# The gate's input turned by VectorE, plain fp32 gate products and the bias on VectorE, in a Fourier mixing and mixture-of-experts kernel

## The chip, the core and the metric

One NeuronCore of a Trainium2 chip runs the whole program. Its engines are TensorE (PE, with its weight loads, PEld), VectorE (DVE), ScalarE (ACT), GpSimd (POOL) and SP, which here only issues DMA transfers. The metric is device time in microseconds (us) of one execution. The kernel before takes 1477.63 us (median of 3 runs, 1476.96 to 1479.51).

## The reference

First a Fourier mixing of x (8 batches, 2496 positions, 256 channels), then a mixture of 8 experts whose routing fills each expert to its capacity in the order of the logits.

```python
X = np.fft.rfft(x, axis=1)
Yr = Xr @ w_r - Xi @ w_i + b_r
Yi = Xr @ w_i + Xi @ w_r + b_i
Yr = np.sign(Yr) * np.maximum(np.abs(Yr) - 0.01, 0.0)      # Yi alike
y = np.fft.irfft(Yr + 1j * Yi, n=2496, axis=1)
logits = y @ w_gate                                        # 19968 x 8
for idx in np.argsort(-logits.flatten()):                  # token, expert by falling logit
    ...                                                    # assign if the token is free and the expert not full
out[mask] = np.maximum(y[mask] @ w1[e], 0.0) @ w2[e]       # for each expert e, 2496 tokens
```

The logits decide the order, so they are computed to fp32 accuracy: in the kernel before by three bf16 parts of y and three of w_gate.

## The kernel before

**Stages of a batch.** The transform of 2496 = 39 x 64 points is done in parts. Stage 1 (line 1168) multiplies x by a matrix of 39 points and goes through DRAM (T1). Stage 3 (line 1208) does the 64 points, frequency by frequency. Then the weights: lines 1227 and 1235 form three products of the complex multiplication, each from a high and a low part of the input (xTh, xTl) and of the weights. VectorE adds them (line 1240) and shrinks them towards zero (1243 to 1246). Stage 4 (line 1256) and, after another trip through DRAM (T2), stage 5 (line 1294, in the last batch the plain fp32 form, line 1287) bring them back to y. Stage 5 works in 11 *units* of a batch, each 2 x 117 positions (the last 117 + 39) by 256 channels, in one PSUM tile. ScalarE copies the unit to yst (line 1296), SP stores it to YD.

**The gate.** TensorE transposes yst by an identity, four products a unit (line 1314), into a PSUM tile of its own (pT). ScalarE rounds that to bf16 (line 1318), VectorE takes the rest (1319), ScalarE (in the last batch VectorE, 1323) rounds the rest (1321), and GpSimd, in batches 1, 5 and 7 VectorE (the tuple YLV), takes the third part (1325). After every fourth unit and after the last, line 1336 multiplies: six rounds, in each of which up to four units stand in four column strips of 32 outputs of TensorE (8 experts x 3 parts of w_gate, 24 outputs). ScalarE copies the logits (1343), SP stores them to LG, unit by unit (1345).

**The bias.** In batches 0, 2, 3, 4 (the tuple BV) VectorE adds it to the products in PSUM (line 1229); in the others TensorE starts the sum with a product of ones and the bias in bf16 parts (line 1223).

**Routing and experts.** SP loads the logits of a batch in two transfers (line 410), VectorE adds the three parts for each pair of batches (417, 418) and takes the maximum. From the first four batches, 512 tokens of every expert are chosen early (`Router.early`), so that the experts can start on them while batches 5 to 7 are still transformed; eight closing rounds choose the rest, each in a chain of small VectorE operations, while TensorE multiplies for the experts (lines 710, 729, 730).

**What sets the order.** A planner written into the kernel (`Plan.run`) takes every task with a cost, a due position (`pos`, made of the numbers in Q) and a slack, fills the buffers and fixes the order of each engine when the program is built; engines then run their rows strictly in that order and wait by semaphores. PSUM has 8 banks, given out by QUOTA.

## Time and profile before

| | us |
|---|---|
| median of 3 runs | 1477.63 |
| profiled execution | 1477.74 |
| its span, first to last instruction | 1475.9 |
| TensorE busy | 1449.2 (98%) |
| VectorE busy | 1131.0 (77%) |
| ScalarE busy | 888.7 (60%) |
| GpSimd busy | 525.2 (36%) |

Busy time is the union of an engine's instructions. Records of matmuls overlap, since they are pipelined, so what one costs is read from the distance between starts and not from its length. The transforms and the gate fill the first 590 us, the experts the rest. TensorE's granted clock was 0.997 of full speed over the span.

### The profile page before, as it was taken

The page shows a single profiled execution, that of the slowest core. Times are in us where ns is not written, and L with a number is a line of the kernel's source. Part 1 is how long each engine was busy: PE and PEld are TensorE (multiplying, and loading weights), DVE is VectorE, ACT ScalarE, POOL GpSimd, SP SyncE. Part 2 cuts the span into 40 slices and gives each one's busy share as a digit, 9 for nine tenths or more (in the row PEclk, how much of TensorE's full clock was granted, in tenths as well). Part 3 has the DMA queues.
Part 4 walks back from the last instruction along what each step waited for, and adds up shares of the span by engine and source line. Part 5 has one row for each costly group of instructions (what it writes and reads, how often), then busy time and mean ns, then how long its engine had stood idle before and what let it go on. Part 6 is the DMA issues. An engine that isn't in the chain of part 4 may idle for free.

```text
span 1475.9 us, 32728 instructions
## 1 busy us (share of the span) xinstructions
PE 1449.2 (98%) x9135; PEld 1221.8 (83%) x9142; DVE 1131.0 (77%) x3234; ACT 888.7 (60%) x2092; POOL 525.2 (36%) x497
## 2 busy tenths in 40 slices
...
GB/s 199 205 316 247 281 213 293 226 283 231 232 231 251 205 172 193 159 119 104 169 136 110 169 109 180 123 161 138 133 118 141 113 118 143 113 67 42 24 22 30
DMA packets 221994, 240.50 MB, mean 163 GB/s; under 512 B 97598, under 2 KB 183787, under 8 KB 221803
## 3 DMA queue, kind: packets, MB, share of 16 engines
...
q14 instruction: 117, 0.96, 0.2%
...
## 4 chain that ended last, share of the span: by engine, by line
PE 85%; DVE 7%; ACT 3%; DMA 2%; issue 2%; SPq 1%; POOL 0%; POOLq 0%; DVEq 0%; ACTq 0%
PE b L710 23%; PE b L729 15%; PE b L730 8%; PE b L1227 7%; PE b L1256 5%; PE b L1208 4%; PE b L1235 4%; PE b L1168 3%; PE b L1294 3%; PE pt L710 3%; PE pt L729 2%; PE b L1314 2%; PE pt L730 1%; PE b L732 1%; PE b L1336 1%
## 5 line engine op out<-in xcount | busy, mean ns | idle before, releaser
L1038 POOL TENSOR_TENSOR s2l<-s2c,s2h 120x512 fp32r<-120x512 f32 (+1 forms) x84 | 105.0, 1256 | 257.9 <-ACT s2h L1035 246.9
L1227 PE MATMUL b<-wt,xTh 128*128 128x256 f32 x640 | 128.3, 297 | 0.9 <-ACT xTh L1214 0.9
L742 POOL DMA_INDIRECT out_dram<-xTh,li x64 | 65.2, 1018 | 158.5 <-DVE xTh L739 97.5
L1227 PEld LDWEIGHTS b<-wt,xTh 128*128 128x128 f32 x640 | 103.1, 191 | 6.5 <-issue 1.4
L742 POOL DMA_INDIRECT out_dram<-xTl,li x64 | 66.0, 1032 | 101.8 <-DVE xTl L739 56.9
L1325 POOL TENSOR_TENSOR yTl<-yr,yTh 128x468 bf16<-128x468 f32 (+1 forms) x55 | 61.3, 1115 | 102.5 <-ACT yTh L1321 79.1
L1208 PE MATMUL b<-FG,sh 128*128 128x128 f32 x640 | 92.2, 278 | 1.2 <-DVE sh L1189 1.2
L1227 PE MATMUL b<-wt,xTl 128*128 128x256 f32 x320 | 91.9, 287 | 1.3 <-DVE xTl L1217 1.3
L1208 PEld LDWEIGHTS b<-FG,sh 128*128 128x128 f32 x640 | 82.7, 191 | 6.3 <-issue 2.4
L738 ACT COPY xTh<-b 128x256 f32<-128x256 f32 x66 | 24.7, 374 | 95.2 <-PE b L730 76.6
L1256 PE MATMUL b<-y,FG 64*128 64x256 f32 x640 | 80.6, 390 | 0.1
L1240 DVE TENSOR_TENSOR y<-b,sx 128x512 f32<-128x512 f32 x80 | 54.9, 688 | 27.1 <-ACT sx L1238 24.2
L1256 PEld LDWEIGHTS b<-y,FG 64*128 64x128 f32 x640 | 58.3, 186 | 12.8 <-issue 1.3
L1168 PE MATMUL b<-xh,d 117*120 117x512 f32 (+1 forms) x154 | 64.2, 423 | 2.3 <-ACT xh L1035 2.2
L1294 PE MATMUL b<-s2h,d 120*117 120x512 f32 (+1 forms) x168 | 65.9, 399 | 0.0
L1319 DVE TENSOR_TENSOR yr<-b,yTh 128x468 f32<-128x468 f32 (+1 forms) x88 | 54.8, 625 | 13.9 <-ACT yTh L1318 13.0
L1038 DVE TENSOR_TENSOR xl<-xt,xh 117x512 fp32r<-117x512 f32 (+1 forms) x77 | 56.8, 747 | 11.0 <-ACT xh L1035 10.7
L1235 PE MATMUL b<-wt,xTh 128*128 128x256 f32 x320 | 63.4, 291 | 0.0
L1227 PEld LDWEIGHTS b<-wt,xTl 128*128 128x128 f32 x320 | 60.8, 190 | 3.1 <-DVE xTl L1217 2.7
...
L738 ACT COPY xTl<-b 128x256 f32<-128x256 f32 x68 | 25.4, 373 | 53.8 <-PE b L730 39.9
L739 DVE TENSOR_TENSOR xTh<-b,xTh 128x256 f32<-128x256 f32 x66 | 27.6, 418 | 38.8 <-ACT xTh L738 36.4
(1229 smaller groups left out, 5275.1 us busy)
## 6 DMA issues: line engine op xcount, KB each, us to landing
...
```

The costliest lines, as they stand in the source:

```text
L710: T.matmul(ps.t[:, 0:w], lhsT=W1[m].t[:, a, 128 * ft:128 * ft + 128], rhs=x_.t[:, 0:w], start=q + m == 0, stop=q + m == 3)
L729: T.matmul(ps.t, lhsT=hh.t[:, u:u + 128], rhs=W2[ft // 4].t[:, :, ft % 4], start=ft == 0, stop=False)
L730: T.matmul(ps.t[:, 0], lhsT=hl.t[:, u:u + 128], rhs=w_[0], start=False, stop=ft == 7)
L742: ins = P.indirect_dma_start(out=self.out, out_offset=bass.IndirectOffsetOnAxis(ap=oi.t[0:M, oo + t:oo + t + 1], axis=0), in_=o.t[0:M], in ...
L1038: lambda: eng.tensor_tensor(lb[1](), src(), hb[1](), op=OP.subtract), [srcb, hb[0]], [lb[0]], port=True)
L1168: T.matmul(ps.t[0:M], lhsT=d1[0:k_, a, 0:M], rhs=v.t[0:k_], start=i == 0, stop=i == 2)
L1208: T.matmul(ps.t[:, :, dt, i], lhsT=sh[k // 8].t[:, k % 8, 128 * dt:128 * dt + 128], rhs=at(Ft, k), start=True, stop=True)
L1227: T.matmul(pc.t[:, c], lhsT=a.t[:, 1 - c, dt], rhs=wt[2 - c].t[:, w, dt], start=not pb and dt == 0 and a is th and w == 0, stop=(c == 1 or ...
L1235: T.matmul(pa.t, lhsT=a.t[:, 2, dt], rhs=wt[0].t[:, w, dt], start=dt == 0 and a is th and w == 0, stop=dt == 1 and a is tl)
L1256: T.matmul(ps4[i].t[:, r], lhsT=at(Gt, 2 * (p - 1 + r) + c)[h], rhs=zs[r].t[h, c], start=c == 0, stop=c == 1)
L1294: T.matmul(ps.t[0:M, gs_], lhsT=d5[0:k_, a, 0:M], rhs=v.t[0:k_, gs_], start=i == 0, stop=i == 2)
L1325: yq.append(plan.add('V' if on else 'P', dve(2 * W) if on else pool(2 * W), pos + Q['t5'], lambda yh=yh, yl=yl, yr=yr, W=W, on=on: (V if o ...
```

## The change

VectorE turns each unit of y straight from the PSUM tile of stage 5 with one transpose of 32 x 32 blocks. After it, partition 32q + c holds channel c of every block of 32 channels, for the rows 32q to 32q + 31 of the unit; so the gate needs eight products a unit, one for each block of channels, with weights that are a block diagonal (the 32 x 8 piece of w_gate four times). They are plain fp32, 64 columns wide, up to four units side by side in column strips. The transposes on TensorE, their tile pT and the three bf16 parts of y and of w_gate are gone, and with them the additions of logit parts. Stage 5 writes 128 partitions, the last eleven zero. The logits lie in LG in another order: 24 stores instead of 88 and six loads a batch (`logit_parts`) instead of two. VectorE adds the bias in all batches; the bf16 bias and its preparation are gone. All numbers of the planner are new (of Q, P1X and SLACK two lines are shown), and buffers of the old gate serve the experts under the name ex.

```diff
-    D1 = np.zeros((117, 120)); D5 = np.zeros((120, 117))
+    D1 = np.zeros((117, 120)); D5 = np.zeros((120, 128))
...
-P1X = -8.145
+P1X = -9.511
...
-SLACK = dict(split=1.661, count=0.243, back=0.303, lists=0.8, os=1.437, hid=0.28, mm4=0, mm4l=0.807, tr=0.477, trl=2.345, gate=0.682, gatel=2.407)
+SLACK = dict(split=1.565, count=0.366, back=0.155, lists=0.715, os=1.464, hid=0, mm4=0.149, mm4l=1.175, tr=1.717, trl=3.296, gate=1.037, gatel=2.447)
...
-YLV = (1, 5, 7)
...
+TU = .62
...
-def load_logits(K, H, LG, LGb, b, lo, pos):
+def logit_parts(ML, LG, b):
     q, h = b // 2, b % 2
-    for t, r, n, w in ((H.ML[64 * h:64 * h + 64, :, JP * q:JP * q + JP], 0, 8, H.b_ML), (None, 8, 16, lo)):
-        K.dma(pos, lambda t=t, r=r, n=n: K.nc.sync.dma_start(lo.t[64 * h:64 * h + 64] if t is None else t, LG[b, r:r + n].rearrange("v (p j) -> p v j", j=JP)), 80e3, [LGb[b]], [w], run=156)
-
-
-def route_prep(K, H, q, lo, pos):
+    for c in range(3):
+        n = 22 if not c else 21
+        for k in range(2):
+            a, e = (JP * c, 32 * c + 32) if not k else (32 * c + 32, JP * c + JP)
+            if e > a: yield ML[64 * h + c:64 * h + c + 3 * n - 2:3, :, JP * q + a - JP * c:JP * q + e - JP * c], LG[b, a // 32].rearrange("e (n t) -> n e t", t=32)[0:n, :, a % 32:(e - 1) % 32 + 1]
+
+
+def load_logits(K, H, LG, LGb, b, pos):
+    def load():
+        for t, src in logit_parts(H.ML, LG, b): K.nc.sync.dma_start(t, src)
+    K.plan.add('SP', 2.4, pos, load, [LGb[b]], [H.b_ML], load=moved(80e3, 100, late=LATE['sp']))
+
+
+def route_prep(K, H, q, pos):
...
-    v(8 * JP, pos(), lambda: V.tensor_tensor(lo.t[:, 0:8], lo.t[:, 0:8], lo.t[:, 8:16], op=OP.add), [lo], [lo])
-    v(8 * JP, pos(), lambda: V.tensor_tensor(H.ML[:, :, J], H.ML[:, :, J], lo.t[:, 0:8], op=OP.add), [H.b_ML, lo], [H.b_ML])
...
-BV = (0, 2, 3, 4)
 BANKS = [f"b{i}" for i in range(7)] + ["pt0"]
-QUOTA = dict(p1=2, pz=2, p5=2, ps2=2, ps3=2, pa=1, ps4=2, pT=2, pL=1, psh=3, pl=1, pso=2, psx=1, pq=1)
+QUOTA = dict(p1=2, pz=2, p5=2, ps2=2, ps3=2, pa=1, ps4=2, pL=1, psh=3, pl=1, pso=2, psx=1, pq=1)
...
-    Bd1, Bd5, Bwg = K.one("d1", [117, 2, 120], F32R), K.one("d5", [120, 2, 117], F32R), K.one("wg", [128, 2, 32], BF)
+    Bd1, Bd5, Bwg = K.one("d1", [117, 2, 120], F32R), K.one("d5", [120, 2, 128], F32R), K.one("wg", [128, 8, 32])
...
-        r1, r2, bh = sb("y2", [128, 2, 256]), sb("xl", [128, 2, 256]), sb("s2h", [128, 2, 256], BF)
         plan.add('V', dve2(512), -1.4, lambda: V.tensor_scalar(Bbf.t, Bbt.t, LAM, None, op0=OP.add), [Bbt], [Bbf], after=after)
-        for q, (u, v) in enumerate(((Bbf, r1), (r1, r2))):
-            plan.add('V', dve2(512), 6.0, lambda u=u: V.tensor_copy(bh.t, u.t), [u], [bh], after=after)
-            plan.add('V', dve(512), 6.0, lambda u=u, v=v: V.tensor_tensor(v.t, u.t, bh.t, op=OP.subtract), [u, bh], [v], after=after)
-        plan.add('V', dve2(512), 6.0, lambda: V.tensor_scalar(Bbt.t, Bbf.t, idn[:, 0:1], None, op0=OP.mult), [Bbf, r1, Bidn], [Bbt], after=after)
-        plan.add('V', dve(512), 6.0, lambda: V.scalar_tensor_tensor(Bbt.t, r1.t, idn[:, 1:2], Bbt.t, op0=OP.mult, op1=OP.add), [Bbt, r1, r2, Bidn], [Bbt], after=after)
-        plan.add('V', dve(512), 6.0, lambda: V.scalar_tensor_tensor(Bbb.t, r2.t, idn[:, 2:3], Bbt.t, op0=OP.mult, op1=OP.add), [Bbt, r2, Bidn], [Bbb], after=after)
-        gs = sb("sx", [128, 2, 8])
-        plan.add('V', dve(64), -14, lambda: V.memset(wg, 0.0), [], [Bwg])
-        wl.append(add_dma(-79, lambda: nc.sync.dma_start(gs.t, w_gate.rearrange("(t p) e -> p t e", p=128)), 8e3, [], [gs], run=32, late=0))
-
-        g = gs
-        for k in range(3):
-            plan.add('V', dve(16), 5, lambda k=k, g=g: V.tensor_copy(wg[:, :, 8 * k:8 * k + 8], g.t), [g], [Bwg], after=after)
-            if k == 2: break
-            rest = sb("sx", [128, 2, 8])
-            plan.add('V', dve(16), 5, lambda k=k, g=g, rest=rest: V.tensor_tensor(rest.t, g.t, wg[:, :, 8 * k:8 * k + 8], op=OP.subtract), [g, Bwg], [rest], after=after)
-            g = rest
+        z_ = plan.add('V', dve(256), -14, lambda: V.memset(wg, 0.0), [], [Bwg])
+        for q in range(4): wl.append(add_dma(-79, lambda q=q: nc.sync.dma_start(wg[32 * q:32 * q + 32, :, 8 * q:8 * q + 8], w_gate.rearrange("(m c) e -> c m e", c=32)), 8e3, [], [Bwg], after=[z_], run=32, late=0))
...
-            pb = b not in BV
-
-            def mmc(th=th, tl=tl, pc=pc, pb=pb):
-                if pb: T.matmul(pc.t, lhsT=Bone.t, rhs=Bbb.t, start=True, stop=False)
+            def mmc(th=th, tl=tl, pc=pc):
                 for c in range(2):
                     for dt in range(2):
                         for a, w in ((th, 0), (th, 1), (tl, 0)):
-                            T.matmul(pc.t[:, c], lhsT=a.t[:, 1 - c, dt], rhs=wt[2 - c].t[:, w, dt], start=not pb and dt == 0 and a is th and w == 0, stop=(c == 1 or not pb) and dt == 1 and a is tl)
-            plan.add('T', 1.67 if pb else 1.44, pos + Q['m3'], mmc, [th_, tl_] + [Bone, Bbb] * pb + wt[1:], [pc], uses=[th, tl])
-            if not pb: plan.add('V', dve(512), pos + Q['zz'] - Q['ba'], lambda pc=pc: V.tensor_tensor(pc.t, pc.t, Bbf.t, op=OP.add), [pc, Bbf], [pc])
+                            T.matmul(pc.t[:, c], lhsT=a.t[:, 1 - c, dt], rhs=wt[2 - c].t[:, w, dt], start=dt == 0 and a is th and w == 0, stop=dt == 1 and a is tl)
+            plan.add('T', 1.44, pos + Q['m3'], mmc, [th_, tl_] + wt[1:], [pc], uses=[th, tl])
+            plan.add('V', dve(512), pos + Q['zz'] - Q['ba'], lambda pc=pc: V.tensor_tensor(pc.t, pc.t, Bbf.t, op=OP.add), [pc, Bbf], [pc])
...
-            ps = psum("p5", [117, 2, 256])
+            ps = psum("p5", [128, 2, 256])
...
-            W = 234 if u < 10 else 156
-            psT = psum("pT", [128, 2, 234])
-            yh, yl, yr = sb("yTh", [128, 2, 2, 234], BF), sb("yTl", [128, 2, 234], BF), sb("yr", [128, 2, 234])
-
-            def tr(u=u, st=st, psT=psT):
-                for i in range(2):
-                    M = 117 if u < 10 or i == 0 else 39
-                    for dt in range(2):
-                        T.transpose(psT.t[:, dt, 117 * i:117 * i + M], st.t[0:M, i, 128 * dt:128 * dt + 128], idn[0:M, 0:M])
-            plan.add('T', 0.44, pos + Q['t5'], tr, [st, Bidn], [psT], after=turn, slack=SLACK['trl' if b == NB - 1 else 'tr'])
-
-            y1_, y2_ = vb(), vb()
-            yt.append(plan.add('A', act(2 * W), pos + Q['t5'], lambda yh=yh, psT=psT, W=W: A.copy(yh.t[:, 0, :, 0:W], psT.t[:, :, 0:W]), [psT], [yh, y1_], after=yt[-1:]))
-            plan.add('V', dve(2 * W), pos + Q['t5'], lambda yh=yh, yr=yr, psT=psT, W=W: V.tensor_tensor(yr.t[:, :, 0:W], psT.t[:, :, 0:W], yh.t[:, 0, :, 0:W], op=OP.subtract), [psT, y1_], [yr])
-            if b < NB - 1:
-                plan.add('A', act(2 * W, False), pos + Q['t5'], lambda yh=yh, yr=yr, W=W: A.copy(yh.t[:, 1, :, 0:W], yr.t[:, :, 0:W]), [yr], [yh, y2_])
-            else:
-                plan.add('V', dve2(2 * W), pos + Q['t5'], lambda yh=yh, yr=yr, W=W: V.tensor_copy(yh.t[:, 1, :, 0:W], yr.t[:, :, 0:W]), [yr], [yh, y2_], port=True)
-            on = b in YLV
-            yq.append(plan.add('V' if on else 'P', dve(2 * W) if on else pool(2 * W), pos + Q['t5'], lambda yh=yh, yl=yl, yr=yr, W=W, on=on: (V if on else P).tensor_tensor(yl.t[:, :, 0:W], yr.t[:, :, 0:W], yh.t[:, 1, :, 0:W], op=OP.subtract), [yr, y2_], [yl], after=yq[-1:], port=True))
-
-            ys.append((yh, yl, W))
+            yT = sb("yT", [128, 2, 8, 32])
+            yt.append(plan.add('V', TU, pos + Q['t5'], lambda yT=yT, ps=ps: V.transpose(yT.t.rearrange("p g m r -> p (g m r)"), ps.t.rearrange("p g e -> p (g e)")), [ps], [yT], after=yt[-1:]))
+            ys.append(yT)
             if u % 4 < 3 and u < 10: continue
-            psL = psum("pL", [128, 234])
-            lg = sb("lgst", [128, 234])
-            u0 = u - len(ys) + 1
+            psL = psum("pL", [128, 2, 32])
+            lg = sb("lgst", [128, 2, 32])
+            u0, n = u - len(ys) + 1, len(ys)
 
             def gt(ys=ys, psL=psL):
-                for n in range(6):
+                for m in range(8):
                     for g, y in enumerate(ys):
-                        T.matmul(psL.t[32 * g:32 * g + 32, 0:y[2]], lhsT=wg[:, n % 2], rhs=y[1].t[:, n % 2, 0:y[2]] if n > 3 else y[0].t[:, n // 2, n % 2, 0:y[2]], start=n == 0, stop=n == 5)
-            plan.add('T', 0.47 + .12 * len(ys), pos + Q['g5'], gt, [t for y in ys for t in y[0:2]] + [Bwg], [psL], slack=SLACK['gatel' if b == NB - 1 else 'gate'])
-            for g, y in enumerate(ys):
-                w, M = y[2], 32
-                if w == 234:
-                    if g: continue
-                    M = 32 * sum(1 for y in ys if y[2] == 234)
-                plan.add('A', act(w), pos + .8, lambda g=g, M=M, w=w, lg=lg, psL=psL: A.copy(lg.t[32 * g:32 * g + M, 0:w], psL.t[32 * g:32 * g + M, 0:w]), [psL], [lg])
-            for g, y in enumerate(ys):
-                add_dma(pos + Q['lg'], lambda c0=234 * (u0 + g), g=g, w=y[2], lg=lg: nc.sync.dma_start(LG[b, :, c0:c0 + w], lg.t[32 * g:32 * g + 24, 0:w]), 22e3, [lg], [LGb[b]], run=936)
+                        T.matmul(psL.t[32 * g:32 * g + 32], lhsT=wg[:, m], rhs=y.t[:, :, m], start=m == 0, stop=m == 7)
+            plan.add('T', 1.1, pos + Q['g5'], gt, ys + [Bwg], [psL], slack=SLACK['gatel' if b == NB - 1 else 'gate'])
+            plan.add('A', act(64), pos + .8, lambda n=n, lg=lg, psL=psL: A.copy(lg.t[0:32 * n], psL.t[0:32 * n]), [psL], [lg])
+
+            add_dma(pos + Q['lg'], lambda n=n, c=64 * u0, lg=lg: nc.sync.dma_start(LG[b].rearrange("q e t -> (q e) t")[:, c:c + 64 * n].rearrange("k (g t) -> g k t", g=n), lg.t[0:32 * n].rearrange("k i t -> k (i t)")), 8e3 * n, [lg], [LGb[b]], run=256)
...
-    H.end = yq[-1:] if IOTA else []
+    H.end = yt[-1:] if IOTA else []
...
-    LG = dram.tile([B, 24, S], F32, name="LG")
+    LG = dram.tile([B, 4, 8, 704], F32, name="LG")
```

**TensorE, where units are transposed** (first stage-5 units of the first batches). Before, line 1314 is the transposes of a unit, line 1294 stage 5, line 1208 stage 3:

```order
L1294 MATMUL b_1655<-s2h_1487,d_96 117x512
L1294 MATMUL b_1655<-s2l_1511,d_96 117x512
L1294 MATMUL b_1655<-s2h_1487,d_96 117x512
L1314 MATMUL b_1662<-h_idn,yst_1561 128x117 x4
L1208 MATMUL b_1669<-FG_188,sh_1046 128x2x64 x4
L1294 MATMUL b_1682<-s2h_1564,d_96 117x512
L1294 MATMUL b_1682<-s2l_1577,d_96 117x512
```

In the changed kernel, with line 1280 for stage 5, 1158 for stage 1 and 1198 for stage 3, the same place reads:

```order
L1280 MATMUL b_1549<-s2h_1440,d_96 128x512
L1280 MATMUL b_1549<-s2l_1455,d_96 128x512
L1280 MATMUL b_1549<-s2h_1440,d_96 128x512
L1198 MATMUL b_1558<-FG_194,sh_1034 128x2x64 x4
L1280 MATMUL b_1574<-s2h_1508,d_96 128x512
L1280 MATMUL b_1574<-s2l_1519,d_96 128x512
L1280 MATMUL b_1574<-s2h_1508,d_96 128x512
L1158 MATMUL b_1586<-xh_1451,d_95 120x512
L1158 MATMUL b_1586<-xl_1537,d_95 120x512
```

The four transposes behind a stage-5 product are gone and nothing stands for them on TensorE.

**TensorE, the first gate.** Before, the bias product (line 1223), a group of weights products (1227) and the first of 24 pairs of weight load and gate product (1336):

```order
L1223 LDWEIGHTS h_ones
L1223 MATMUL b_1718<-bb,h_ones 128x512
L1227 MATMUL b_1718<-wt_305,xTh_1692 128x256 x2
L1227 MATMUL b_1718<-wt_305,xTl_1706 128x256
L1227 MATMUL b_1718<-wt_305,xTh_1692 128x256 x2
L1227 MATMUL b_1718<-wt_305,xTl_1706 128x256
L1227 MATMUL b_1718<-wt_291,xTh_1692 128x256 x2
L1227 MATMUL b_1718<-wt_291,xTl_1706 128x256
L1227 MATMUL b_1718<-wt_291,xTh_1692 128x256 x2
L1227 MATMUL b_1718<-wt_291,xTl_1706 128x256
L1336 LDWEIGHTS wg
L1336 MATMUL b_1750<-yTh_1413,wg 32x234
```

In the changed kernel, weights products (now line 1214) and the first four of 32 gate products (1303); the loads of fp32 weights are part of the rows:

```order
L1214 MATMUL b_1640<-wt_306,xTh_1591 128x256 x2
L1214 MATMUL b_1640<-wt_306,xTl_1612 128x256
L1214 MATMUL b_1640<-wt_306,xTh_1591 128x256 x2
L1214 MATMUL b_1640<-wt_306,xTl_1612 128x256
L1214 MATMUL b_1640<-wt_292,xTh_1591 128x256 x2
L1214 MATMUL b_1640<-wt_292,xTl_1612 128x256
L1214 MATMUL b_1640<-wt_292,xTh_1591 128x256 x2
L1214 MATMUL b_1640<-wt_292,xTl_1612 128x256
L1303 MATMUL b_1670<-yT_1371,wg 32x64
L1303 MATMUL b_1670<-yT_1415,wg 32x64
L1303 MATMUL b_1670<-yT_1510,wg 32x64
L1303 MATMUL b_1670<-yT_1563,wg 32x64
```

The bias product is gone from the head of the weights products, and a gate of four units is 32 rows over four inputs instead of 24 over eight.

**VectorE, batch 5's units beside batch 6's splits.** Before, with lines 1319 and 1325 for the parts of y, 1215 to 1218 for the splits of stage 3's output, 1240 for the sum of the weights products, the other lines early routing:

```order
L1319 TENSOR_TENSOR yr_6830<-b_6793,yTh_6825 128x468
L817 TENSOR_TENSOR ge_6747<-ge_6747,ga_6819 128x78
L549 TENSOR_SCALAR RD_6821<-ga_6771,wi_6800 128x78
L556 TENSOR_SCALAR Sme_6839<-h_io,wi_6800 128x512
L1218 TENSOR_TENSOR xTl_6778<-sx_6743,xTh_6745 128x256
L1325 TENSOR_TENSOR yTl_6848<-yr_6830,yTh_6825 128x468
L1215 TENSOR_TENSOR sx_6846<-b_6787,sx_6846 128x256
L1217 TENSOR_TENSOR xTl_6862<-b_6787,xTh_6850 128x512
L1218 TENSOR_TENSOR xTl_6862<-sx_6846,xTh_6850 128x256
L1240 TENSOR_TENSOR y_6880<-b_6802,sx_6743 128x512
L1319 TENSOR_TENSOR yr_6899<-b_6867,yTh_6878 128x468
```

In the changed kernel, with line 1293 for the block transpose, 1205 to 1208 for the splits, 1216 for the bias, 1230 for the shrinking, 651 for an expert's weights:

```order
L1227 TENSOR_TENSOR y_6215<-b_6133,sx_6034 128x512
L1293 STREAM_TRANSPOSE yT_6227<-b_6179 128x512
L1205 TENSOR_TENSOR sx_6229<-b_6210,sx_6229 128x256
L1207 TENSOR_TENSOR xTl_6242<-b_6210,xTh_6231 128x512
L1293 STREAM_TRANSPOSE yT_6250<-b_6236 128x512
L1208 TENSOR_TENSOR xTl_6242<-sx_6229,xTh_6231 128x256
L871 COPY h_lohi<-st_6131 128x1
L894 TENSOR_TENSOR rng<-h_lohi 128x1
L1230 SCALAR_TENSOR_TENSOR y_6215<-y_6215,y_6272 128x512
L1216 TENSOR_TENSOR b_6257<-b_6257,bf 128x512
L651 TENSOR_TENSOR sp_6286<-xt_6085,sp_6286 128x512 x2
```

One transpose stands where two subtractions stood, and an addition of the bias has come between a batch's products and their sum.

## Rows read from the trace of the kernel before

**Rows 1.** The page, part 1: busy us, share of span, instructions.

```profile
PE 1449.2 (98%) x9135; PEld 1221.8 (83%) x9142; DVE 1131.0 (77%) x3234; ACT 888.7 (60%) x2092; POOL 525.2 (36%) x497
```

**Rows 2.** Busy time by stretch; columns in the first row, (x) counts instructions.

```profile
core 0: us, PE busy (x) PEld busy (x) DVE busy (x) ACT busy (x) POOL busy (x), PEclk, DMA share, GB/s
0.00:394.00 394.00, 385.45 (x3008) 333.86 (x3014) 303.98 (x577) 326.05 (x725) 112.46 (x100) 1.00 0.78 251
394.00:599.00 205.00, 199.74 (x1550) 163.41 (x1552) 183.75 (x514) 167.36 (x419) 79.50 (x70) 1.00 0.66 205
700.00:800.00 100.00, 99.27 (x526) 80.63 (x525) 96.99 (x327) 57.42 (x152) 43.98 (x42) 1.00 0.45 143
```

**Rows 3.** TensorE's timeline around a gate: start, us, operation, count.

```profile
129.70 0.40 PE L1227 MATMUL b<-wt,xTh 128*128 128x256 f32 x2
129.94 0.28 PE L1227 MATMUL b<-wt,xTl 128*128 128x256 f32 x1
130.15 0.59 PE L1336 MATMUL b<-yTh,wg 128*32 128x234 bf16 x16
130.57 0.37 PE L1336 MATMUL b<-yTl,wg 128*32 128x234 bf16 x8
130.87 0.62 PE L1314 MATMUL b<-h_idn,yst 117*128 117x117 f32 x4
```

**Rows 4.** TensorE's timeline around the transposes of a unit.

```profile
105.21 0.56 PE L1314 MATMUL b<-h_idn,yst 117*128 117x117 f32 x4
105.64 0.58 PE L1227 MATMUL b<-wt,xTh 128*128 128x256 f32 x2
```

**Rows 5.** TensorE's timeline around a bias product (line 1223).

```profile
84.63 0.38 PE L1223 MATMUL b<-bb,h_ones 128*128 128x512 bf16 x1
84.85 0.50 PE L1227 MATMUL b<-wt,xTh 128*128 128x256 f32 x2
85.90 0.39 PE L1227 MATMUL b<-wt,xTl 128*128 128x256 f32 x1 [0.55 <-DVE xTl L1217]
```

**Rows 6.** Single lines: engine, operation, count: ns min/median/max, first and last start, forms.

```profile
L1314 PE MATMUL b<-h_idn,yst x352: 227/263/321, 105.2 to 577.1; 117*128 117x117 f32 x168, 39*128 39x39 f32 x8
...
L1336 PEld LDWEIGHTS <-wg x528: 92/97/100, 130.1 to 585.0; 128*32 128x32 bf16 x176
...
L1223 PEld LDWEIGHTS <-h_ones x40: 95/97/100, 84.5 to 523.5; 128*128 128x128 bf16 x40
```

**Rows 7.** The chain of waits in order of time: start, us, what (two stretches).

```profile
107.41 1.93 PE b L1256 x16
...
546.94 1.72 PE b L1287 x4
```

**Rows 8.** VectorE by line and form: count, busy us, mean ns, idle before.

```profile
L1319 DVE TENSOR_TENSOR yr<-b,yTh 128x468 f32<-128x468 f32 x80 | 51.1, 640 | 13.9 <-ACT yTh L1318 13.0 <-issue 0.5
...
L1229 DVE TENSOR_TENSOR b<-b,bf 128x512 f32<-128x512 f32 x40 | 27.7, 694 | 3.2 <-PE b L1227 3.1
...
L1325 DVE TENSOR_TENSOR yTl<-yr,yTh 128x468 bf16<-128x468 f32 x30 | 20.0, 670 | 1.5 <-PE b L1336 1.2
...
L1323 DVE CAST yTh<-yr 128x468 bf16<-128x468 f32 x10 | 3.9, 404 | 0.1
...
L418 DVE TENSOR_TENSOR h_ML<-h_ML,lo 128x312 f32<-128x312 f32 x4 | 2.8, 699 | 0.0
...
L417 DVE TENSOR_TENSOR lo<-lo 128x312 f32<-128x312 f32 x4 | 2.5, 616 | 0.2 <-DMA lo<-LG 0.2
...
L681 DVE STREAM_TRANSPOSE yTl<-yTh 128x256 f32<-128x256 f32 x4 | 1.7, 437 | 0.0
```

**Rows 9.** VectorE's waits, 0 to 590 us: total us, times, longest.

```profile
DVE sx L1215 <- ACT xTh L1214: 20.3, 33, 1.8
```

**Rows 10.** SP's logit transfers, by line (columns as in rows 6).

```profile
L1345 SPq DMA_DIRECT2D LG<-lgst x88: 289/362/1091, 131.4 to 587.0; - x88
...
L410 SPq DMA_DIRECT2D h_ML<-LG x8: 586/590/1102, 189.7 to 588.5; - x8
```

More of the change, by code (lines that the diff above doesn't have):

```diff
@@ L999, in phase_a @@
     k4 = lambda p, i: p // 2 * 4 + p % 2 + 2 * i
-    Bd1, Bd5, Bwg = K.one("d1", [117, 2, 120], F32R), K.one("d5", [120, 2, 117], F32R), K.one("wg", [128, 2, 32], BF)
+    Bd1, Bd5, Bwg = K.one("d1", [117, 2, 120], F32R), K.one("d5", [120, 2, 128], F32R), K.one("wg", [128, 8, 32])
     d1, d5, wg, idn, Bidn = Bd1.t, Bd5.t, Bwg.t, H.idn, H.b_idn
-    Bd5f = K.one("d5f", [120, 117])
-    Bml, Bone, Bbb = K.one("ml", [128, 1]), H.b_ones, K.one("bb", [128, 2, 256], BF)
+    Bd5f = K.one("d5f", [120, 128])
+    Bml, Bone = K.one("ml", [128, 1]), H.b_ones
     Bbf = K.one("bf", [128, 2, 256])
@@ L1064, in load_consts @@
             GX.append(add_dma(-80 + q, lambda k0=k0, k1=k1, G=G, o=o: nc.sync.dma_start(G.t[:, k0 - o:k1 - o], cG[:, k0:k1, :]), 65e3 * (k1 - k0), [], [G, BG_[q]], run=512 * (k1 - k0), late=0))
-        es = sb("yr", [120, 2, 117])
-        GX.append(add_dma(-70, lambda: nc.sync.dma_start(es.t, cD5.rearrange("p (h m) -> p h m", h=2)), 112e3, [], [es], run=936, k=15, late=12))
-        plan.add('V', dve(234), 9, lambda: V.tensor_copy(d5, es.t), [es], [Bd5])
+        es = sb("yT", [120, 2, 128])
+        GX.append(add_dma(-70, lambda: nc.sync.dma_start(es.t, cD5.rearrange("p (h m) -> p h m", h=2)), 112e3, [], [es], run=1024, k=15, late=12))
+        plan.add('V', dve(256), 9, lambda: V.tensor_copy(d5, es.t), [es], [Bd5])
         fg[:] = FX, GX
@@ L1265, in batch @@
         lg, ys = None, []
-        turn = yt[-1:] if b == NB - 1 else []
         for u in range(NU):
@@ L1286, in batch @@
                 if plain:
-                    plan.add('T', 4 * n / 2400, pos, lambda c_=c_, ps=ps, gs_=gs_, k_=k_, M=M: T.matmul(ps.t[0:M, gs_], lhsT=d5f[0:k_, 0:M], rhs=c_.t[0:k_, gs_], start=True, stop=True), [c_, Bd5f], [ps])
+                    plan.add('T', 4 * n / 2400, pos, lambda c_=c_, ps=ps, gs_=gs_, k_=k_: T.matmul(ps.t[:, gs_], lhsT=d5f[0:k_], rhs=c_.t[0:k_, gs_], start=True, stop=True), [c_, Bd5f], [ps])
                 else:
@@ L1290, in batch, with mm @@
                           (h, lambda h=h, gs_=gs_, k_=k_: h.t[0:k_, gs_]), (l, lambda l=l, gs_=gs_, k_=k_: l.t[0:k_, gs_]), 'A', 'P', n)
-                    def mm(h=h, l=l, ps=ps, gs_=gs_, k_=k_, M=M):
+                    def mm(h=h, l=l, ps=ps, gs_=gs_, k_=k_):
                         for i, (a, v) in enumerate(((0, h), (0, l), (1, h))):
-                            T.matmul(ps.t[0:M, gs_], lhsT=d5[0:k_, a, 0:M], rhs=v.t[0:k_, gs_], start=i == 0, stop=i == 2)
+                            T.matmul(ps.t[:, gs_], lhsT=d5[0:k_, a], rhs=v.t[0:k_, gs_], start=i == 0, stop=i == 2)
                     plan.add('T', 3 * (.004 + .000446 * n), pos, mm, [h, l, Bd5], [ps])
@@ L1346, in batch @@
             ys = []
-    last_sh, yt, yq = [], [], []
+    last_sh, yt = [], []
     head, wl, fg = [], [], []
```

30 lines of the change are left out of this document (12 added, 18 removed).

## The prediction

> **What bounds the kernel now.** I read the engine totals first, then the busy time by stretch, then TensorE's own timeline. TensorE is busy 98% of the span [rows 1]. By stretch it never rests for long: 385.45 of the first 394 us, 199.74 of the next 205, 99.27 of 100 later [rows 2]. No wait of TensorE stands among the long waits, so it is bound by the sum of what it is given, and an instruction taken off it shortens the span unless another engine is too full to follow. The reader should therefore look at the runner-up: VectorE is busy 303.98 of 394, then 183.75 of 205 us, and 96.99 of 100 in a later stretch in which TensorE still has 99.27 [rows 2]. The frequency transforms with the gate end at about 590 us; the change lies wholly before that.
>
> Busy times of single TensorE rows overlap, so I price work by the distance between starts. The gate of four units: the two weights products from 129.70 to 129.94 take 0.12 us each, the last one before the gate starts at 129.94 and so ends its turn at 130.06, the next work starts at 130.87: 0.81 us [rows 3]. Four transposes of a unit: 105.21 to 105.64, 0.43 us [rows 4]. A bias product: 84.63 to 84.85, 0.22 us [rows 5].
>
> **What leaves TensorE.** The trace has 352 transposes, four to a unit, so 88 units [rows 6]: 88 x 0.43 = 37.8 us; one unit in eleven is smaller, I take 37. It has 528 gate products [rows 6] in 24 groups (three to a batch, eight batches; a group of three units has as many rounds as one of four): 24 x 0.81 = 19.4 us. The 40 bias products (batches 1, 5, 6, 7) [rows 6] are 40 x 0.22 = 8.8 us at most. Here the cover matters: behind one of them a weights product stands 0.55 us for the low part of its input, which VectorE makes [rows 5]; there, without the bias, TensorE would only begin to wait sooner. Ends 0 and 8.8; I take 5. Sum: 37 + 19.4 + 5 = 61.4 us.
>
> **What comes to TensorE.** 24 groups of 8 fp32 products for each unit, 64 columns wide, 32 outputs high, four units in four column strips. The trace holds no fp32 product in a column strip, so I bound it. An fp32 product appears in the trace as two matmuls. The chain of waits has 4 matmuls of 512 columns in 1.72 us [rows 7]: 0.43 us for 512, hence 0.054 us for 64 columns; with a start-to-start allowance I use 0.056. With the strips side by side a group is 8 x 2 = 16 rounds of 0.056 = 0.90 us. The old gate shows the rest: six rounds of about 0.10 us are 0.6 of its 0.81, so entering and leaving strip mode costs 0.2. New group: 1.10 us. Do fp32 matmuls run side by side at all? In half-height tiles they do: 16 of 256 columns take 1.93 us, 0.12 each, where the 512-column rate gives 0.215 [rows 7]. Lower end 0.90, upper end 64 matmuls one after another, 64 x 0.056 + 0.2 = 3.8 us. I take 1.10, the value nearest to the rows that do overlap: 24 x 1.10 = 26.4 us. **Net on TensorE: 61.4 - 26.4 = 35.0 us less.** The stage-5 products now fill 128 outputs instead of 117; their columns, and so their turns, are the same.
>
> The weight loads of the gate are where a rule speaks against this change. The trace has 528 of them at 97 ns [rows 6], 24 in a group of 0.81 us: laid end to end they would be 2.3 us, so they are hidden behind running strips. The Trainium skill, TensorE: Matmul & The Clock Gate, Part 3 (Packing small matmuls), says that "LDWEIGHTS overlaps with in-flight MATMULs only when row_grp differs"; column strips share all rows, so by it no load would be hidden. The bf16 gate disagrees with that rule; for fp32 strips no run here shows it yet. The rule's result is the second rival.
>
> **VectorE.** It loses 88 subtractions of about 0.64 us, 33 of 0.67 (batches 1, 5, 7), 11 casts of 0.40, and eight additions of logit parts (2.5 + 2.8 us) [rows 8], together 56 + 22 + 4 + 5 = 87 us. It gains 40 additions of the bias at 0.694 [rows 8], 27.8 us, and 88 block transposes of 512 elements from PSUM. The nearest rows are a transpose of 256 elements from SBUF, 437 ns, and an addition of 512 elements from PSUM, 694 ns [rows 8]; ends 0.44 and 0.87 (twice the smaller one), I take 0.70: 61.6 us. Over the stage VectorE is even: +89 against -87.
>
> But it moves towards the end. In the later part, 394 to 599 us, in which about batches 4 to 7 are finished, the gain is 30 bias additions, 20.8 us, and 33 x 0.06 for the longer transposes; the loss is 22 subtractions (14.7), the casts (4) and half the logit additions (2.6): +1.5, so 185.2 us. The four batches in it lose 4 x 35/8 = 17.5 us of TensorE, so the stretch would be 187.5 us with VectorE 99% full. At the 97% that it reaches elsewhere without holding TensorE [rows 2] it needs 190.9: **3.4 us come back.** If it could not be filled beyond today's 183.75/205 = 90%, 206 us would be needed and the whole 17.5 would come back.
>
> **New waits.** ScalarE's copy of y and VectorE's transpose now read the same PSUM tile. Engines take turns on one: VectorE's line 1215 waited 33 times, 20.3 us, for ScalarE's line 1214 on the tile that both read [rows 9]. Behind a waiting transpose on VectorE stand the splits and bias additions for the next weights products. In exchange the subtraction that waited for ScalarE's copy of the old transposes goes. I cost this at 0, ends -4 and +6, hidden by the distance between transposing and gating (the planner puts whole products between them). The last batch's copies no longer follow one another through ScalarE and VectorE before the last gate; that only helps the start of the routing.
>
> **Transfers.** SP issues 24 logit stores instead of 88 (0.36 us each) and 48 loads instead of 16 (0.59) [rows 10]: 32 + 9 = 41 us of issuing before, 9 + 28 = 37 after if the new ones cost the same. The pieces are short, down to 28 bytes, but only the last batch's are waited for; ends 0 and 2 us, I take 0, because VectorE has other work then.
>
> **Sum.** The profiled execution took 1477.74 us (span 1475.9), 0.1 above the median of 1477.63, so no correction. 1477.74 - 35.0 + 3.4 = 1446.1: I forecast **1446 us**.
>
> **The rivals.** (1) *VectorE becomes the bound of the second half.* For it: 90% full already, 30 additions more there. Against: 97% elsewhere without harm. Price: 17.5 instead of 3.4 us come back: 1460 us. (2) *Weight loads are not hidden in fp32 strips.* Each of 16 rounds pays a load of 0.097 us beside its 0.056: 16 x 0.153 + 0.2 = 2.65 us a group, 63.6 in all, against 61.4 saved: 1477.74 + 2.2 + 3.4 = 1483 us, a little slower. Against it: the old gate's hidden loads. (3) *The strips run one after another in fp32*, at the gate itself: 3.8 us a group, 91 us, 1477.74 - 61.4 + 91 + 3.4 = 1511 us, slower. Both decide from 2.56 us a group (61.4/24); beyond that the change loses. Against (3): the fp32 half-height pairs. (4) *The work goes but the new order waits*: all but some microseconds lost to buffers and turns on PSUM, 1466 to 1480.
>
> **How the numbers follow.** Forecast 0.68, (1) 0.16, (2) 0.05, (3) 0.04, (4) 0.07. Within 0.2% (3 us) is what a measurement of this kernel can't tell from no change. Faster by more: the forecast, (1) and about half of (4), 0.88. Same: 0.03. Slower: (2), (3), and a little of (4), 0.09. The lower bound: all 8.8 us of bias, 37.8 of transposes, nothing returned: 1477.74 - 39.6 = 1438, less 4 for VectorE's freed waits: 1434. The upper end takes in rival (1) with the 6 us of turns on PSUM: 1466. Left out below about 0.06, above about 0.13.
>
> **What would show it.** In the changed profile: TensorE about 35 us less busy before the routing and still near 98%; a gate group of about 1.1 us between neighbours (2.6 or 3.8 show the rivals); transposes on VectorE near 0.70 us; ScalarE and GpSimd emptier by their copies and subtractions. The prediction is wrong if a gate group passes 2 us, if TensorE waits for VectorE by more than some 10 us in batches 5 to 7, or if the stretch after 600 us (now shifted) grows longer.

## The result and the profile after

The changed kernel took 1453.97 us (median of 4, 1451.99 to 1458.17) against 1478.49 before: a ratio of 0.9837, 95% interval 0.9818 to 0.9856. A second measurement of the same kernel gave 1453.31 us and 0.9842 (0.9827 to 0.9856). The forecast was 1446, with 1434 to 1466 as its range: the direction was right, and 7 to 8 us of the forecast gain of 32 are missing.

There are two profiled executions of the changed kernel: the first of 1458.17 us (span 1456.4), the slowest of its four, and one from the second measurement, 1453.30 us (span 1451.5), at the median. They differ mainly in two early stretches (busy time by stretch, columns as in [rows 2]; the first execution, then the second).

```profile
20.00:25.00 5.00, 4.28 (x38) 4.08 (x37) 1.69 (x4) 2.03 (x5) 0.00 (x0) 1.00 0.96 329
25.00:35.00 10.00, 7.09 (x28) 6.10 (x29) 4.12 (x8) 4.34 (x9) 0.00 (x0) 0.66 0.21 56
85.00:90.00 5.00, 5.00 (x27) 4.72 (x26) 2.14 (x6) 2.18 (x6) 0.00 (x0) 0.66 0.99 376
```

```profile
25.00:35.00 10.00, 7.80 (x46) 6.81 (x47) 5.97 (x11) 5.34 (x12) 0.00 (x0) 0.83 0.20 52
85.00:90.00 5.00, 4.83 (x41) 4.61 (x40) 4.54 (x10) 3.40 (x9) 0.00 (x0) 1.00 1.03 371
```

TensorE's granted clock, a mean of its two levels, is 1.00 at 20 us and 0.66 from 25 to 35 us in the first execution, 0.83 in the second. In between TensorE stood still for ScalarE's first split of batch 1, at about 24 us, 3.6 us long in the first and 3.1 in the second; ScalarE itself was waiting for the transfer of x. The first falls to 0.66 again at 85 us, after another wait at 82 us. At 0.66 instead of 0.83 over 10 us, and instead of 1.00 over 5, it lacks 1.7 + 1.7 = 3.4 us of full speed; the spans differ by 4.9. I therefore measure by the second execution, which stands at the median as the profiled run of before did. Its engine totals, to be laid beside [rows 1]:

```profile
PE 1418.9 (98%) x9630; PEld 1198.2 (83%) x9630; DVE 1118.2 (77%) x3210; ACT 813.1 (56%) x1919; POOL 470.8 (32%) x442
```

TensorE is busy 30.3 us less (1449.2 before). The span less this busy time is 32.6 us, 26.7 before. So 30.3 us of work went and 5.9 us of idle came: 24.4 us, which is the difference of the spans. The forecast had 35.0 and 3.4.

**The gate.** TensorE's timeline around the first gate of the second execution (start, us, operation, count), to be laid beside [rows 3]:

```profile
125.02 0.28 PE L1214 MATMUL b<-wt,xTl 128*128 128x256 f32 x1
125.22 1.10 PE L1303 MATMUL b<-yT,wg 128*32 128x64 f32 x64
126.25 0.51 PE L1222 MATMUL b<-wt,xTh 128*128 128x256 f32 x2
```

The product before the gate ends its 0.12 us turn at 125.14 and the next work starts at 126.25: 1.11 us, where 1.10 was forecast. The rivals had 2.65 and 3.8. A group has 64 weight loads, here by line in the first execution (columns as in [rows 6]):

```profile
L1303 PEld LDWEIGHTS b<-yT,wg x1408: 106/110/110, 129.3 to 570.0; 128*32 128x32 f32 x176
```

**VectorE.** By line and form, first execution, 0 to 600 us (count, busy, mean ns, idle before):

```profile
L1293 DVE STREAM_TRANSPOSE yT<-b 128x512 f32<-128x512 f32 x87 | 61.5, 709 | 8.3 <-PE b L1273 4.5 <-ACT yst L1282 1.8 <-PE b L1280 1.3
L1216 DVE TENSOR_TENSOR b<-b,bf 128x512 f32<-128x512 f32 x80 | 55.3, 692 | 12.5 <-PE b L1214 12.5
```

A block transpose is 709 ns; 0.70 was taken. Its idle time for ScalarE's copy of the same PSUM tile is 1.8 us, and TensorE waits for a transpose once, 0.5 us, so nothing here speaks against the 0 that was put down for the turns on PSUM. The SP queue's two logit transfers, to be laid beside [rows 10], were dearer than assumed:

```profile
L1307 SPq DMA_DIRECT2D LG<-lgst x24: 534/556/797, 131.7 to 570.8; - x24
...
L418 SPq DMA_DIRECT2D h_ML<-LG x48: 734/746/1043, 177.9 to 578.8; - x48
```

That is 13.3 + 35.8 = 49 us of issuing, not 37, and 41 before. No wait of TensorE names them.

**The new idle time.** TensorE's waits from 0 to 600 us (total us, times, longest); before first, the changed kernel (second execution) below it.

```profile
PE b L1168 <- ACT xh L1035: 2.2, 1, 2.2
PE pt L471 <- DVE cnt L466: 1.8, 2, 1.1
PE b L1227 <- DVE xTl L1217: 1.3, 3, 0.6
```

```profile
PE b L1214 <- DVE xTl L1207: 5.7, 11, 1.4
PE b L1158 <- ACT xh L1041: 4.1, 2, 3.1
PE b L1222 <- DVE xTl L1208: 1.8, 3, 1.4
```

The weights products now wait for the low part of their input, which VectorE subtracts: 5.7 us and eleven times, where it was 1.3 us and three times. The longest is read on both engines, TensorE first:

```profile
450.78 0.49 PE L1214 MATMUL b<-wt,xTh 128*128 128x256 f32 x2
452.64 0.39 PE L1214 MATMUL b<-wt,xTl 128*128 128x256 f32 x1 [1.38 <-DVE xTl L1207]
```

```profile
448.29 0.69 DVE L1216 TENSOR_TENSOR b<-b,bf 128x512 f32<-128x512 f32 x1
448.89 2.17 DVE L1230 SCALAR_TENSOR_TENSOR y<-y,y 128x512 f32<-128x512 f32 x1
450.98 0.68 DVE L1227 TENSOR_TENSOR y<-b,sx 128x512 f32<-128x512 f32 x1
451.58 0.41 DVE L1205 TENSOR_TENSOR sx<-b,sx 128x256 f32<-128x256 f32 x1
451.91 0.67 DVE L1207 TENSOR_TENSOR xTl<-b,xTh 128x512 fp32r<-128x512 f32 x1
```

```profile
449.21 1.29 POOL L1044 TENSOR_TENSOR s2l<-s2c,s2h 120x512 fp32r<-120x512 f32 x1
```

TensorE stands still because VectorE is behind: the subtraction at 451.91 comes after a bias addition and one operation, of line 1230, that took 2.17 us. GpSimd was subtracting beside it from 449.21 to 450.50 (the last line). The 35 operations of line 1230 that met no such subtraction took 0.68 us each; the last experiment comes back to this.

### The profile page after: what moved, and what is told of

Its sections match the earlier page's. It is cut to its first block, busy times and chain, and to the rows that moved or that the text cites. A ratio compares the mean times of both kernels' runs of the same rounds, so it can differ in the third digit from the quotient of the medians.

```text
span 1456.4 us, 33431 instructions
## 1 busy us (share of the span) xinstructions
PE 1422.1 (98%) x9630; PEld 1200.7 (82%) x9630; DVE 1119.2 (77%) x3210; ACT 813.3 (56%) x1919; POOL 473.3 (32%) x442
## 4 chain that ended last, share of the span: by engine, by line
PE 79%; DVE 13%; DMA 3%; ACT 2%; issue 2%; SPq 0%; POOL 0%; POOLq 0%; DVEq 0%; ACTq 0%
PE b L717 23%; PE b L736 15%; PE b L737 8%; PE b L1214 6%; PE b L1243 4%; PE b L1198 3%; PE pt L717 3%; PE b L1222 3%; PE b L1158 3%; PE pt L736 3%; PE b L1280 2%; PE pt L737 1%; PE b L1303 1%; DMA xt<-in_x_dram 1%; DVE xTl L1207 1%
## 5 line engine op out<-in xcount | busy, mean ns | idle before, releaser
L1214 PE MATMUL b<-wt,xTh 128*128 128x256 f32 x640 | 125.1, 291 | 0.0
L1293 DVE STREAM_TRANSPOSE yT<-b 128x512 f32<-128x512 f32 x87 | 61.5, 709 | 8.3 <-PE b L1273 4.5
L1280 PE MATMUL b<-s2h,d 120*128 120x512 f32 (+1 forms) x168 | 66.4, 404 | 0.0
L1216 DVE TENSOR_TENSOR b<-b,bf 128x512 f32<-128x512 f32 x80 | 55.3, 692 | 12.5 <-PE b L1214 12.5
L580 ACT ACTIVATE ajunk<-b,h_bs 128x156 bf16<-128x156 f32 x122 | 47.7, 391 | 27.5 <-PE b L575 23.1
L1282 ACT COPY yst<-b 117x512 f32<-117x512 f32 (+2 forms) x95 | 52.2, 557 | 19.4 <-DVE yT L1293 12.6
L1222 PE MATMUL b<-wt,xTh 128*128 128x256 f32 x320 | 62.9, 288 | 0.0
L717 PE MATMUL b<-yT,sh 128*128 128x512 f32 (+1 forms) x170 | 61.3, 384 | 0.0
```

Source lines behind the costliest of these rows:

```text
L717: T.matmul(ps.t[:, 0:w], lhsT=W1[m].t[:, a, 128 * ft:128 * ft + 128], rhs=x_.t[:, 0:w], start=q + m == 0, stop=q + m == 3)
L1214: T.matmul(pc.t[:, c], lhsT=a.t[:, 1 - c, dt], rhs=wt[2 - c].t[:, w, dt], start=dt == 0 and a is th and w == 0, stop=dt == 1 and a is tl)
L1222: T.matmul(pa.t, lhsT=a.t[:, 2, dt], rhs=wt[0].t[:, w, dt], start=dt == 0 and a is th and w == 0, stop=dt == 1 and a is tl)
L1280: T.matmul(ps.t[:, gs_], lhsT=d5[0:k_, a], rhs=v.t[0:k_, gs_], start=i == 0, stop=i == 2)
L1293: yt.append(plan.add('V', TU, pos + Q['t5'], lambda yT=yT, ps=ps: V.transpose(yT.t.rearrange("p g m r -> p (g m r)"), ps.t.rearrange("p g ...
```

## The experiments

Each run was measured beside the kernel before on the same chip. Where "the changed kernel" is the yardstick it is the second measurement, 1453.31 us; a cost is a difference of medians.

**The yardstick** (the changed kernel again).

> The changed kernel unchanged, as the yardstick of this call. Profiled first it took 1458.17 us, its median of four was 1453.97. Theory (waits that hang on the moment a transfer lands come and go): the median stays at 1452 to 1456, and the two longest early waits (3.9 us at 24 us, 2.2 us at 82 us) are shorter in another profile, while the waits of batch 7's weights products stay. Rival (the profile's 1458 is the truth): 1457 to 1459.

Measured 1453.31 us, 0.9842 (0.9827 to 0.9856). The theory held: both early waits are shorter (from start to start 3.4 instead of 3.9 us at 24 us, 1.4 instead of 2.2 at about 80 us) and the clock after them is higher, while the waits of the weights products are the same 5.7 and 1.8 us. The first profile's 1458 is the same kernel with longer early waits.

**Bias back on TensorE in four batches.** The table of its three addends occupies one of the five spare slots for expert data.

```
-            plan.add('V', dve(512), pos + Q['zz'] - Q['ba'], ...pc.t + Bbf.t...)
+            pb = b in (1, 5, 6, 7)
+                if pb: T.matmul(pc.t, lhsT=Bone.t, rhs=Bbb.t, start=True, stop=False)
+            if not pb: plan.add('V', dve(512), pos + Q['zz'] - Q['ba'], ...pc.t + Bbf.t...)
```

> The changed kernel with the bias of batches 1, 5, 6 and 7 again made by a TensorE product, as in the kernel before; VectorE adds it in batches 0, 2, 3, 4 only. Theory (removing these 40 products was worth nothing, because the products behind them wait for the low part from VectorE anyway, and VectorE's 30 additions after 394 us cost more waits): no slower than the changed kernel, 1448 to 1455 us, and the weights products of batch 7 wait at least 3 us less. Rival (the bias products cost what the forecast put down, 5 us, up to 8.8): 1459 to 1463 us.

Measured 1454.75 us, 0.9837 (0.9823 to 0.9850): no difference. The totals of its profile, and two of TensorE's waits to 600 us (its lines 1225 and 1215 are 1214 and 1207 of the changed kernel):

```profile
PE 1423.7 (98%) x9667; PEld 1202.2 (83%) x9670; DVE 1096.2 (75%) x3177; ACT 813.4 (56%) x1919; POOL 470.9 (32%) x442
```

```profile
PE b L1225 <- DVE xTl L1215: 3.7, 8, 1.2
...
PE b L1225 <- ACT xTh L1212: 0.8, 1, 0.8
```

TensorE is busy 4.8 us more, close to the 5 that the forecast had put down for these products, and idle 1453.2 - 1423.7 = 29.5 us instead of 32.6. From 440 to 540 us, about where batch 7 is, the waits for low parts fall by 2.3 us (4.8 to 2.5), short of the 3 that the theory wanted. This run moves work on two engines: TensorE has 40 products more, VectorE 22 us less to do. It shows that the exchange is worth nothing that the noise lets one see; what the products cost by themselves is read from the run without any bias, below.

**Bias back on TensorE in batch 7 alone** (the same edit with `b in (7,)`).

> The changed kernel with the bias of batch 7 alone again by TensorE: 10 products come back to it, 10 additions of 0.69 us leave VectorE between about 456 and 530 us. Theory (the waits of batch 7 are VectorE's doing): 3 to 5 us faster than the changed kernel, 1449 to 1451. Rival (each bias product costs TensorE its 0.13 to 0.22 us and the waits stay): 1 to 2 us slower.

Measured 1453.58 us, 0.9837 (0.9823 to 0.9850): neither. The waits of these products for the low part are 5.7 us as before; the one at 451 us is 1.2 instead of 1.4 us, and one of 1.5 us has grown at 503 us. The 1.8 us of the neighbouring products (line 1222) are gone. So batch 7's own ten additions account for about a third of its waits at most (4.8 to 3.2 us from 440 to 540 us), and ten products on TensorE stand against that.

**The old tables of numbers in the changed kernel** (`P1X`, `SLACK` and `Q` as before).

> The changed kernel with the three tables of planner numbers of the kernel before (lead, slack and due times). The work is the changed kernel's, only its order is other. Theory (the gain is the work taken from TensorE, the tables are worth a few us): 1456 to 1466 us, still faster than before. Rival (the gain comes from the new numbers): 1475 or more.

Measured 1458.50 us, 0.9862 (0.9847 to 0.9877). Of the 25 us the new numbers are worth about 5, the work 20. The new numbers in the kernel before were not run.

**The gate, one strip after another.**

```
-                for m in range(8):
-                    for g, y in enumerate(ys):
+                for g, y in enumerate(ys):
+                    for m in range(8):
```

> The changed kernel with the 64 TensorE records of a gate group in another order: all eight products of one unit (one column strip), then of the next, instead of the four strips in turn. Nothing else moves. Theory (a group costs 1.03 us because the four strips run side by side): products of one strip follow one another at 0.056 us or more, a group takes 3.6 us, 24 groups add some 62 us: 1510 to 1520 us, slower than before; if their weight loads of 0.11 us show as well, 7 us a group and up to 1600. Rival (an fp32 product of 64 columns is cheap by itself, strips or not): 1453 to 1458.

Measured 1488.41 us, 1.0063 (1.0048 to 1.0077): slower than before. The same place of TensorE's timeline:

```profile
125.83 0.28 PE L1214 MATMUL b<-wt,xTl 128*128 128x256 f32 x1
126.04 3.18 PE L1303 MATMUL b<-yT,wg 128*32 128x64 f32 x64
129.15 0.51 PE L1222 MATMUL b<-wt,xTh 128*128 128x256 f32 x2
```

A group goes from 1.03 to 3.11 us between first start and the next work; the records of one strip start 0.056 us apart, the price taken in the prediction. I had expected 3.6, and 62 us on top: start-to-start at the borders of strips falls to 0.025 to 0.030 us, so the next strip begins beside the last. The groups add 43.5 us on TensorE and the time 35. Of the rivals that were to make the change a loss, the one with strips that run one after another would thus have been real; the order of two loops decides it.

**The gate twice** (`for m in [*range(8), *range(8)]`).

> The changed kernel with each gate group computed twice, the second pass over the first. Theory (what TensorE is given sets the time): 0.94 us more in each of 24 groups, 22 us less what waits can hide, 1470 to 1476. Rival (TensorE's waits for VectorE hide the gate): under 1465.

Measured 1471.04 us, 0.9955 (0.9938 to 0.9972): 17.7 us for 23.1 us of groups. Each of the 24 groups takes 1.92 instead of 1.03 us, which is 21.4 us in all; the rest is waits inside a few of them.

**Every block transpose of one half made twice.**

```
+ [V.transpose(yT..., ps...) for _ in range(1 + (b in (0, 1, 2, 3)))]     (the other run: 4, 5, 6, 7)
```

> The changed kernel with each block transpose of batches 0 to 3 made twice by VectorE: 44 x 0.70 = 31 us more on VectorE between about 100 and 360 us, nothing on TensorE. Theory (VectorE at 82% has room there): 0 to 5 us, 1453 to 1458. Rival (VectorE is on the path all through): 1470 or more.

Measured 1470.89 us, 0.9943 (0.9930 to 0.9956). The theory fell, and the rival's number came: 17.6 us for 31 us of VectorE, in the half in which VectorE is 80% busy in the changed kernel (first line, columns as in [rows 2]). TensorE's waits for line 1207 rise from 5.7 to 12.9 us, and their number from 11 to 23 (second line, of this run).

```profile
0.00:394.00 394.00, 382.88 (x3379) 333.12 (x3380) 314.16 (x655) 292.55 (x646) 74.66 (x63) 1.00 0.81 253
```

```profile
PE b L1214 <- DVE xTl L1207: 12.9, 23, 1.4
```

> The changed kernel with each block transpose of batches 4 to 7 made twice by VectorE: 44 x 0.70 = 31 us more between about 360 and 570 us, nothing on TensorE. Theory (VectorE is 89% busy there and its fullness returns part of the gain): the stretch of 186 us holds 165 us of VectorE's work, 196 do not fit, so at least 10 us, and up to 30, come on top: 1464 to 1483. Rival (VectorE has room here as well, and the waits come from the order): under 1458.

Measured 1475.13 us, 0.9978 (0.9968 to 0.9987): 21.8 us for 31.

**The same in the second half, told to the planner** (`TU * (1 + (b > 3))` as its length).

> As the run with the block transposes of batches 4 to 7 made twice, but the planner is told their length of 1.24 us, so that it can put other work around them. Theory (VectorE stands at an edge: what is taken from it is worth 0.1 us per us, what is put on it 0.6 to 0.7, since 165 + 31 us don't fit into that stretch): the cost stays at least 10 us over the changed kernel, 1464 or more. Rival (the 22 us came from an order planned for the shorter transposes): under 1460.

Measured 1470.37 us, 0.9954 (0.9940 to 0.9968): 17.1 us. Planning around it gives 4.8 back (3.5 by the ratios to the kernel before); the other 17 us remain although the planner knew the length. One of its stretches, and below it that of the changed kernel:

```profile
510.00:540.00 30.00, 25.43 (x243) 19.22 (x242) 28.52 (x70) 15.83 (x48) 14.25 (x14) 0.89 0.50 154
```

```profile
510.00:540.00 30.00, 29.31 (x262) 21.34 (x259) 25.42 (x73) 20.94 (x63) 12.76 (x13) 1.00 0.78 217
```

VectorE is busy 28.52 of 30 us, TensorE stands still for 4.6, and its granted clock is 0.89 where it was 1.00. Over 30 us that is 3.3 us of full speed, lost beside the time in which it stands still.

**The bias part alone, in the kernel before** (`BV` with all eight batches).

> The kernel before with one part of the change alone: the bias of batches 1, 5, 6, 7 added by VectorE as in the others, tables of numbers as before. TensorE loses 40 bias products, VectorE gets 40 additions of 0.69 us, 28 us. Theory (a microsecond put on VectorE costs 0.55 to 0.7 us even in the first batches, one taken from TensorE gives back about 0.8): 28 x 0.6 - 5 x 0.8 = 13 us slower, 1485 to 1495. Rival (the forecast's: the 5 us off TensorE show and VectorE swallows the additions): 1473 to 1476 us.

Measured 1484.67 us, 1.0047 (1.0033 to 1.0061): 6 us slower, just under the theory's range and clear of the rival's. By itself, with the tables of the kernel before, this part of the change is a loss.

**No bias at all in batches 1, 5, 6, 7.**

> The changed kernel with no bias in batches 1, 5, 6, 7 at all (left out: the result lacks it there). VectorE loses 40 additions of 0.69 us, 28 us; TensorE loses nothing. It tells what relief of VectorE is worth, against what load on it costs. Theory (doubling the transposes cost 0.57 to 0.71 us per us because they came unplanned in one lump; with the bias on TensorE the time stayed while 3 to 4 us of waits went): 3 to 6 us faster than the changed kernel, 1447 to 1450. Rival (VectorE is worth 0.6 us per us in both directions): 16 us faster, 1435 to 1440.

Measured 1451.18 us, 0.9816 (0.9803 to 0.9829): 2 us faster, less than the theory had, and hardly clear of the noise. Its totals:

```profile
PE 1417.4 (98%) x9630; PEld 1199.1 (83%) x9630; DVE 1096.0 (76%) x3170; ACT 811.6 (56%) x1919; POOL 471.3 (33%) x442
```

Taking 28 us of bias additions off VectorE is worth about 0.1 us a us; putting 31 us of transposes on it cost 0.55 to 0.7. These are different operations in different places, so the two figures do not show that the direction makes the difference.

Against the run with the bias back on TensorE, VectorE has the same work here (1096.0 and 1096.2 us busy), and only the 40 products are missing: 1454.75 - 1451.18 = 3.6 us (3.1 by the ratios, whose intervals just overlap). So the products did cost time, and the additions that replaced them cost 2.1 us.

**Low parts of x on GpSimd.**

```
-                  ..., 'A', 'V', 512)
+                  ..., 'A', 'P' if u % 2 else 'V', 512)
```

> The changed kernel with the low part of x of every second stage-1 unit (35 subtractions of 0.71 us) made by GpSimd, which is 32% busy, instead of VectorE; GpSimd takes about 1.29 us for one of this size. Theory (VectorE is the second bound, and this relieves it by 25 us without work for TensorE): 2 to 8 us faster than the changed kernel, 1445 to 1451. Rival (while GpSimd subtracts, VectorE's own SBUF work is held up, as in the single 2.17 us addition of the trace where others take 0.67): no gain or some us slower, 1453 to 1465.

Measured 1455.45 us, 0.9852 (0.9837 to 0.9867): the rival; no gain. GpSimd took 1.39 us for one, by form in its profile:

```profile
L1044 POOL TENSOR_TENSOR xl<-xt,xh 117x512 fp32r<-117x512 f32 x35 | 48.5, 1385 | 174.5 <-ACT xh L1041 150.4 <-DMA T<-s1st 11.7 <-DMA YD<-yst 9.4
```

VectorE's total fell by 12.6 us (1118.2 to 1105.6) where 35 subtractions of 0.73 are 25. The two traces show where most of the rest went. VectorE's operations on SBUF alone are longer while GpSimd subtracts: those of line 1208 (256 elements) take 0.41 us by themselves; 17 that met a subtraction in this run took 0.79 on average, 9 in the changed kernel 0.94. Those of line 1207, which read PSUM, take 0.68 either way. Summed over all of VectorE's lines, what the operations that met a subtraction took beyond the median of the others of their line is 18 us in the changed kernel and 28 here. So the rival's mechanism is seen in the traces, and it is the likely cause of the 2.17 us operation ahead of TensorE's wait at 451 us; a run without GpSimd's subtractions was not made. No run beat the changed kernel with its bias.

## Why the prediction was right, and where it was not

The mechanism held in the main: time follows the work that TensorE is given (the doubled gate cost 17.7 us for 23.1), and the change takes 36.4 - 7.5, some 29 us, of transposes and gate from it. What failed is the price of the exchange of the bias between the two engines. Term by term, from the start of one product to the start of the next over all records of both traces (the second execution for after):

- Transposes: 36.4 us were there (37 taken).
- The gate: its groups with their way out took 18.1 us before and 25.6 after. The difference of 7.5 answers to 26.4 - 19.4 = 7.0.
- The bias: 5 us was the mis-sized term. As work on TensorE it was there: with the bias the median group of weights products took 1.65 us before, without it takes 1.53 after, and 40 such differences are about 4.9, an estimate. (The 0.22 us of [rows 5] is no typical row: after the other 32 recorded bias products the next start comes within 0.03 to 0.04 us, and the one behind it after 0.31. That 5 met the work was luck.) The prediction saw the cover in that row, a wait of 0.55 us behind the bias product, and took a value between its ends. But weights and bias products together took 195.1 us before and 200.5 after; with the bias back on TensorE they take 201.4, with no bias at all 194.4 (sums of single executions; the changed kernel's other one has 202.3). So the bias costs TensorE about as much when VectorE adds it, in waits, as when TensorE does. In time, the 40 products cost 3.6 us, the 40 additions 2.1, and the exchange is worth 1.4, which the noise covers. The prediction counted the products and, VectorE's sum being even, put nothing beside the next term for the additions.
- What VectorE gives back: 3.4 forecast. I call a distance between starts above 0.48 us long and count what it has beyond 0.48. These long waits of TensorE rose from 12.4 to 17.3 us over the whole span: 4.9. From 394 to 600 us, the stretch that the forecast named, they rose only from 4.3 to 6.2, 1.8 and not 3.4: between 450 and 550 us from 1.5 to 4.8, while from 394 to 450 they fell from 2.5 to 1.1. Another 1.6 came between 100 and 394 us, 0.3 before 100 and 1.1 after 600 us, where it had put nothing. From 450 to 550 us VectorE is busy 89%, not the 97 to 99% that was worked out for the stretch; TensorE waits for single operations of VectorE that are late, before VectorE is full.
- The turns on PSUM and the transfers: 0, and no wait of TensorE speaks against it; no run took them alone.

VectorE's 89% stands in this row of the changed kernel (columns as in [rows 2]):

```profile
450.00:550.00 100.00, 94.24 (x889) 76.46 (x890) 88.97 (x211) 66.30 (x185) 35.27 (x32) 1.00 0.69 205
```

In sum, 36.4 - 7.5 - 4.9 is 24.0, and the spans differ by 24.4. So 0.4 us is left for the bias and all shorter waits together, where 5 was forecast. The differences then add up to the miss: 0.6 and 0.5 for transposes and gate, 1.5 for the long waits and 4.6 for the bias make 7.2, and 1453.3 - 1446.1 is 7.2. Each part comes from one execution, and 0.4 is a remainder, not a measurement of the bias.

The rivals. That VectorE bounds the second half (1460): the time lies half-way between it and the forecast, but not by its mechanism. Long waits grew by 1.8 us in that half, and 28 us less on VectorE gave 2 us. It has a point all the same: the doubled transposes show that work put on VectorE has a price, in both halves, long before it is full, and the forecast gave it none in the first. Weight loads that are not hidden (1483) are ruled out by the gate's 1.11 us. The rule of the Trainium skill, TensorE: Matmul & The Clock Gate, Part 3 (Packing small matmuls), that a load overlaps with a running product only where the row group differs, does not agree with this case, in which all strips share their rows: 64 loads of 0.11 us laid end to end would be 7 us, and a group takes 1.03 us with its strips in turn and 3.11 us even with one strip after another. Strips in series (1511) were not the case here; with one strip after another, each beginning a little before the last ends, it would have been 1488. The new order (1466 to 1480) is ruled out by the old tables: they cost 5 us, the new ones gain them.
